# A shared remainder tile's o by heads in array quadrants, one batch's weighted sums placed later, and idle products moved ahead of kv

## The chip, the cores and the metric

The kernel runs on one core of a Trainium2 chip. The metric is device time in microseconds (us) of one launch, the median of several runs. The kernel before takes 321.6 us (three runs, 321.56 to 321.62).

## What is computed

Inputs are q, k and v of 8 batches, 8 heads, 576 positions and a head size of 64, in float32, and the weights of a gated feed-forward layer.

```python
kv = einsum('bhsd,bhse->bhde', k, v)          # 64 x 64 per batch and head
out = einsum('bhsd,bhde->bhse', q, kv)
out = out / sqrt(mean(out**2, -1) + 1e-6) * g_norm
x = out.transpose(0, 2, 1, 3).reshape(4608, 512)
xn = x / sqrt(mean(x**2, -1) + 1e-6) * rms_g
y = (silu(xn @ w_gate) * (xn @ w_val)) @ w_out      # 512 -> 1536 -> 512
```

There is no softmax, so attention is a small product (kv), a product with q (o), and two normings.

## The kernel before

**Tiles.** A batch's 576 positions are four chunks of 128 and a remainder of 64. The remainders of two batches share one tile of 128 rows, so the feed-forward work is nine groups of 512 rows: eight of the batches' chunks (`x`) and one of all remainders (`xr`). The groups run in the order 0 to 6, the remainders' group, 7.

**Feed-forward.** Per group and block j of 128 hidden columns, `gate_of` and `val_of` (L705, L708) each issue four TensorE products over the 512 rows (`mm1`, L694) into one bank of the PSUM pool `mm1`, which has three buffers. ScalarE applies silu (L703), and VectorE multiplies silu by val into `h` (L712). Then come 48 products with `w_out` (`mm2`, L729) for four out tiles in the pool `o2`, each copied by ScalarE (L745) and stored through SyncE's queue (L747).

**Attention of the next batch runs inside a group.** The class `Att` holds its steps: kv (`kv_mm`, L281: each head's product fills half of the array's columns), q transposed by DMA (L342, and L345 for the shared remainder tile), o of the chunks by heads (`o_heads`, L375: contraction over 64 rows, so that each product uses half of the array's rows; two PSUM tiles of `o2` and two of `att` receive the even and the odd heads), and o of the shared remainder tile (`o_rem`, L362: contraction over 128 rows against the block-diagonal `kvs`, one column half per batch, into one tile of `att`). Batches 2, 3, 5 and 7 carry a remainder tile; batches 4 and 6 do not. Then ScalarE squares (`sq_`, L410) and copies (`outa_`, L414) each chunk of o out of PSUM, GpSimd multiplies the square by the norm gain's square (`wsq`, L465), VectorE sums both per head (`red`, L473), computes the row factors in a chain of small steps (`chain`, L512 to L530), and scales o into `xna` (`xna_`, L540). SyncE's queue transposes `xna` into `x` (`x_dma`, L603), in two pieces and one for a remainder.

**What sets the order.** Each group is a list of slots: a slot is one gate group, one val group, or three products of an out tile. A planner (`Placer`, L40) puts each attention step into the first slot where its engine has room by a table of costs, not earlier than the step's inputs allow. `psum` (L66) does so for a TensorE step and also counts the three buffers of `att`: it lets a step into a slot only when the readers of the tiles that it will overwrite have been placed before. `place_attention` (L617) lists a batch's steps; each engine then executes its instructions in the order of the slots. Within `place_attention`, `o_heads` is one step and `o_rem` another, which comes after a tile of `att` is free; the chunks are squared and copied first and the remainder last.

**The start.** Batch 0 is done ahead of the slots, step by step (L854 to L907). `spin` (L243) issues TensorE products of a zero tile that nobody reads: 18 at the start, and four more in the PSUM tile of the first kv products (`kv_pairs`, L286, called at L860). VectorE casts k's first half (L216) and k's remainder `krT` (L858); then `kv_pairs` multiplies k by v (L297), whose loads go through GpSimd's queue.

Of the kernel before, what the change touches and what calls it, by code (L numbers as in the profile page):

```python
# [10 lines left out]
FP32 = mybir.dt.float32  # L11
BF16 = mybir.dt.bfloat16
# [3 lines left out]
ACT = mybir.ActivationFunctionType  # L16
# [71 lines left out]
def kernel(  # L88
# [12 lines left out]
    nc = tc.nc  # L101
    B, H, S, D = q.shape
# [3 lines left out]
    NC = 4  # L106
    MAIN = 128 * NC
# [10 lines left out]
    pool = lambda name, bufs, **kw: ctx.enter_context(tc.tile_pool(name=name, bufs=bufs, **kw))  # L118
# [2 lines left out]
    rstage = pool("rstage", 2)  # L121
    qkv = pool("qkv", 2)
    outa_p = pool("outa", 6)
    sq_p = pool("sq", 3)
    stat = pool("stat", 2)
    sqT_p = pool("sqT", 1)
    xna_p = pool("xna", 2)
# [32 lines left out]
    krT = consts.tile([128, 2, H, D], BF16, name="remk")  # L160
# [82 lines left out]
    def spin(ps, n):  # L243
        for _ in range(n):
            nc.tensor.matmul(ps, lhsT=idle[:, :128], rhs=idle[:, : ps.shape[-1]], start=True, stop=True, skip_group_check=True)  # L245
# [4 lines left out]
    class Att:  # L250
# [103 lines left out]

        def o_rem(self):

            self.o[NC] = o = att_p.tile([128, H, D], FP32, name="att")
            of = (kvs[2], kvs[1]) if self.b == 2 else (kvs[0], kvs[1])
            for j in range(NS):
                for n in range(2):  # L360
                    at = slice(n * REM, (n + 1) * REM)
                    nc.tensor.matmul(  # L362
                        o[at, 2 * j : 2 * j + 2, :], lhsT=self.qTj[:, j, NC, at], rhs=of[n][:, j, :, :],
                        start=True, stop=True, skip_group_check=True,
                    )

        def o_heads(self):

            for n, (pool_, name) in enumerate(((o2_p, "o2"), (o2_p, "o2"), (att_p, "att"), (att_p, "att"))):
                self.o["main", n] = pool_.tile([128, 2, H // 2, D], FP32, name=name)  # L370
            for c in range(NC):
                for j in range(NS):
                    for half in range(2):
                        rows = slice(half * D, (half + 1) * D)
                        nc.tensor.matmul(  # L375
                            self.o["main", c // 2 * 2 + half][:, c % 2, j, :], lhsT=self.qTj[rows, j, c, :],
                            rhs=self.kv[rows, j, half, :], start=True, stop=True, skip_group_check=True,
                        )

        def part(self, t, n):  # L380

            if n >= NC:
                return t[:, n]
            return t[:, n // 2 * 2 : n // 2 * 2 + 2, n % 2 : H : 2]
# [232 lines left out]
    def place_attention(P, b, casts=(), at=0, chain_at=0):  # L617
        a, start = Att(b), at + 2
        V, A = nc.vector, nc.scalar
        N1 = range(a.chunks)  # L620
        P.floor = max(P.floor, at)
        load = P.put("SP", 0.0, a.qT_dma, casts[:1] if b == 2 else casts)
        qt = [("DMA", load[1] + QT_SLOTS)]
        p = P.psum(1.2, lambda: a.kv_mm(ALL), casts)
        kv = [P.reads(P.put("DVE", 0.4, lambda h=h: a.kv_half(h), [p])) for h in range(2)]
        outs, reds = {}, []
        main = P.psum(0.73, a.o_heads, kv + qt, 2)
        for c in N1:
            p = P.psum(0.3, a.o_rem, kv + qt) if c >= NC else main
            s = P.put("ACT", 0.6, lambda c=c: a.sq_(c), [p])  # L630
            outs[c] = P.put("ACT", 0.6, lambda c=c: a.outa_(c), [p])
            if c >= 2:
                P.tiles[-1 if c >= NC else c - 4] += [s, outs[c]]
            assert outs[c][1] < start + 2 * NF, (b, outs)
            w = P.put("POOL", 1.2, lambda c=c: a.wsq(c, nc.gpsimd), [s])
            reds.append(P.put("DVE", 0.68, lambda c=c: a.red(c, 0), [s]))
            reds.append(P.put("DVE", 0.68, lambda c=c: a.red(c, 1), [w]))
        prev = reds
        for n in range(0, 13, 4):
            prev = [P.put("DVE", 0.8, lambda n=n: [f() for f in a.chain(0, a.chunks)[n : n + 4]], prev, chain_at)]  # L640
        xn = [P.put("DVE", 0.68, lambda c=c: a.xna_(c, V), prev + [outs[c]]) for c in N1]
        put = [P.put("SP", 0.0, lambda c=c: a.x_dma(*c), [xn[c[1] - 1]]) for c in ((0, 2), (2, 4), (4, 5))[: a.chunks - 2]]
        return put[2 if b == B - 1 else 1][1] + X_SLOTS
# [178 lines left out]
    P0, P1 = (0, 1), (2, 3)  # L822
# [28 lines left out]
        else:  # L851
            V.tensor_scalar(out=w[:, s], in0=w[:, s], scalar1=gain[:, s : s + 1], scalar2=None, op0=OP.mult)

    spin(mm1_p.tile([128, MAIN], FP32, name="mm1"), 18)  # L854
    a = Att(0)
    cast_main(0, 1, V, H0)
    cast_main(0, 1, A, H1)
    V.tensor_copy(out=krT[: REM // 2], in_=krst.rearrange("p h (c d) -> p c h d", c=2))  # L858
    cast_main(0, 0, V, cs=(0, 2))
    kva = a.kv_pairs(P0, 4)  # L860
    qa, qb = (a.qT_mm(js, (0, 1)) for js in (P0, P1))
    gT = o2_p.tile([128, NS + 1], FP32, name="o2")
    nc.tensor.matmul(gT, lhsT=grow, rhs=identf, is_transpose=True, start=True, stop=True, skip_group_check=True)
# [7 lines left out]
    for half in range(2):  # L871
        rows = slice(half * D, (half + 1) * D)
# [36 lines left out]
    half = MAIN // 2  # L909
# [50 lines left out]
    P = Placer(slots, 3)  # L960
# [64 lines left out]
```

## Time and profile before

| What | us |
|---|---|
| median of three runs | 321.60 |
| the profiled execution | 321.76 |
| its span in the profile | 320.0 |
| VectorE busy | 169.2 |
| ScalarE busy | 138.0 |
| GpSimd busy | 85.2 |

The profile is of one execution. Its span runs from the first to the last recorded instruction; 1.76 us of the execution's time lie around it. Engines are named PE (TensorE), PEld (its weight loads, which overlap its products), DVE (VectorE), ACT (ScalarE), POOL (GpSimd) and SP (SyncE); a name with a q is an engine's own queue of issues. L362 is line 362 of the kernel. The chain that ended last is followed back from the last instruction: at each step to what released it, or to the instruction before it on its engine. In the rows of the chain an engine's pieces join without a gap, so that the starts of two rows show how long everything between them took.

### The profile page before, as it was taken

What the parts mean: (1) busy time and instruction counts of PE and PEld (TensorE: products, weight loads), DVE (VectorE), ACT (ScalarE), POOL (GpSimd) and SP (SyncE); (2) the same over time, 40 slices, a digit from 0 to 9 for tenths busy, and PEclk for the clock granted to TensorE, in tenths of its full rate; (3) what the DMA queues carried; (4) which work ended last, traced back from release to release, by engine and by line L of the source; (5) the groups of instructions that cost most, each with busy time, mean ns of one, the idle gap of its engine ahead of it and who ended that gap; (6) DMA issues with size and microseconds to landing.
All of it is one profiled execution on the core that took longest, in us unless ns stands there. A gap on an engine that the chain in (4) does not pass through costs nothing.

```text
span 320.0 us, 5497 instructions
## 1 busy us (share of the span) xinstructions
PE 312.8 (98%) x2122; PEld 157.7 (49%) x2122; DVE 169.2 (53%) x381; ACT 138.0 (43%) x254; POOL 85.2 (27%) x105
## 2 busy tenths in 40 slices
PE   8799999999999999999999999999999999999995
PEld 3578865444444444444544444444444444444443
DVE  4565536589749651955186717571778043203410
ACT  1465454596667314632383228322842233223321
POOL 8653430077017400830075007500510000000000
PEclk9999999999999999999999999999999999999999
DMA  8999999999761974498349875964000600040002
GB/s 210 221 203 199 195 231 205 228 209 135 153 197 53 166 155 137 131 166 153 121 128 133 148 153 145 153 127 137 11 3 10 183 21 2 15 107 12 0 33 98
DMA packets 79253, 40.69 MB, mean 127 GB/s; under 512 B 42872, under 2 KB 74748, under 8 KB 79228
## 3 DMA queue, kind: packets, MB, share of 16 engines
q0 software_dynamic: 31200, 14.22, 35.1%
q1 hardware_dynamic: 46544, 25.14, 32.2%
q10 hardware_dynamic: 1484, 0.99, 1.0%
q8 instruction: 16, 0.26, 0.3%
q14 instruction: 9, 0.07, 0.1%
HBM read 37.78 MB, written 9.44 MB: 148 GB/s over the span
## 4 chain that ended last, share of the span: by engine, by line
PE 91%; DMA 8%; issue 0%; DVE 0%; ACT 0%; POOLq 0%
PE mm L694 57%; PE o L729 27%; DMA wv<-in_moe_w_val_dram 5%; DMA remv<-in_v_dram 2%; PE att L281 2%; PE mm L729 2%; PE o L375 1%; PE att L375 0%; PE att L362 0%; PE mm L756 0%; PE o L756 0%; PE att L571 0%; PE att L327 0%; PE att L423 0%; PE att L350 0%
## 5 line engine op out<-in xcount | busy, mean ns | idle before, releaser
L712 DVE TENSOR_TENSOR h<-silu,mm 128x512 bf16<-128x512 bf16 (+1 forms) x120 | 75.5, 631 | 86.9 <-PE mm L694 77.0
L703 ACT ACTIVATE silu<-mm 128x512 bf16<-128x512 f32 (+1 forms) x120 | 66.4, 556 | 86.4 <-PE mm L694 75.3
L694 PE MATMUL mm<-x,wv 128*128 128x512 bf16 (+1 forms) x432 | 99.9, 356 | 0.2 <-DMA wv<-in_moe_w_val_dram 0.2
L694 PE MATMUL mm<-x,wg 128*128 128x512 bf16 (+1 forms) x420 | 97.9, 358 | 0.0
L729 PE MATMUL o<-wo,h 128*128 128x512 bf16 x396 | 90.1, 379 | 0.0
L694 PEld LDWEIGHTS <-wv 128*128 128x128 bf16 x480 | 46.2, 98 | 45.7 <-DMA wv<-in_moe_w_val_dram 0.5
L694 PEld LDWEIGHTS <-wg 128*128 128x128 bf16 x468 | 45.1, 98 | 45.7 <-DMA wg<-in_moe_w_gate_dram 0.2
L465 POOL TENSOR_TENSOR sq<-sq,g 128x512 bf16<-128x512 bf16 x28 | 32.0, 1154 | 129.0 <-ACT sq L410 129.0
L729 PEld LDWEIGHTS <-h 128*128 128x128 bf16 x420 | 40.3, 98 | 46.5
L745 ACT COPY osb<-o 128x512 f32<-128x512 f32 x33 | 19.3, 587 | 69.1 <-PE o L729 69.1
L473 DVE TENSOR_REDUCE st<-sq 128x8 f32<-128x512 bf16 x56 | 35.9, 678 | 0.2
L310 DVE CAST kvs<-att 64x256 bf16<-64x256 f32 x14 | 5.9, 422 | 31.9 <-PE att L281 31.7
L540 DVE TENSOR_TENSOR xna<-outa,al 128x512 bf16<-128x512 bf16 x24 | 15.0, 683 | 0.0
L694 PE MATMUL mm<-xr,wg 128*128 128x512 bf16 x48 | 12.3, 379 | 0.0
L694 PE MATMUL mm<-xr,wv 128*128 128x512 bf16 x48 | 12.3, 379 | 0.0
L216 POOL CAST main_q<-stg 128x1024 bf16<-128x1024 f32 (+1 forms) x12 | 11.4, 996 | 1.1 <-DMA stg<-in_q_dram 1.1
L245 PE MATMUL mm<-idle 128*128 128x512 bf16 x27 | 9.0, 505 | 1.2 <-DVE idle L138 1.2
L410 ACT ACTIVATE sq<-att 128x512 bf16<-128x512 f32 x16 | 9.8, 615 | 0.0
L414 ACT CAST outa<-att 128x512 bf16<-128x512 f32 x16 | 9.6, 600 | 0.0
L850 ACT ACTIVATE wv<-wv,gain 128x384 bf16<-128x384 bf16 x16 | 9.0, 608 | 0.4 <-PE mm L694 0.4
L200 POOL DMA_DIRECT2D vc<-in_v_dram x9 | 7.8, 872 | 1.1 <-PE mm L694 1.1
L729 PE MATMUL mm<-wo,h 128*128 128x512 bf16 x24 | 7.8, 379 | 0.0
(132 smaller groups left out, 175.1 us busy)
## 6 DMA issues: line engine op xcount, KB each, us to landing
out_dram<-osb SPq DMA_DIRECT2D x31, 256.0 KB, 2.5
stg<-in_q_dram SPq DMA_DIRECT2D x6, 1024.0 KB, 7.5
vc<-in_v_dram POOLq DMA_DIRECT2D x7, 512.0 KB, 8.2
kc<-in_k_dram POOLq DMA_DIRECT2D x7, 512.0 KB, 6.2
wg<-in_moe_w_gate_dram POOLq DMA_DIRECT2D x4, 384.0 KB, 14.9
wv<-in_moe_w_val_dram POOLq DMA_DIRECT2D x4, 384.0 KB, 16.3
wo<-in_moe_w_out_dram POOLq DMA_DIRECT2D x4, 384.0 KB, 14.7
out_dram<-osb SPq DMA_DIRECT2D x9, 128.0 KB, 2.3
```

Source lines behind the costliest of these rows:

```text
L216: return copy(out=mains[b, t][:, cs[0] : cs[1], h0:h1, :], in_=staged[b, t].rearrange("p h (c d) -> p c h d", c=NC)[:, cs[0] : cs[1], h0:h ...
L245: nc.tensor.matmul(ps, lhsT=idle[:, :128], rhs=idle[:, : ps.shape[-1]], start=True, stop=True, skip_group_check=True)
L410: nc.scalar.activation(out=self.sq[c][:, 0], in_=self.o_of(c), func=ACT.Square)
L414: nc.scalar.copy(out=self.outa[c], in_=self.o_of(c))
L465: eng.tensor_tensor(out=self.sq[c][:, 1], in0=self.sq[c][:, 0], in1=g2, op=OP.mult)
L473: nc.vector.reduce_sum(out=self.part(self.st[:, which], c), in_=of, axis=AX.X)
L540: return eng.tensor_tensor(out=self.part(self.xna, c), in0=self.outa[c].rearrange("p (c h) d -> p c h d", c=2), in1=self.part(self.al, c). ...
L694: nc.tensor.matmul(ps[:, : c1 - c0], lhsT=w[n][:, s, jj * 128 : (jj + 1) * 128], rhs=x_of(g, s, c0, c1), start=s == 0, stop=s == NS - 1)
L703: nc.scalar.activation(out=sis[g, j][:, c0:c1], in_=ps, func=ACT.Silu)
L712: nc.vector.tensor_tensor(out=hs[g, j][:, c0:c1], in0=sis[g, j][:, c0:c1], in1=v_ps, op=OP.mult)
L729: nc.tensor.matmul(ps, lhsT=hs[g, j][:, t * 128 : (t + 1) * 128], rhs=wo[j // OB][:, j % OB, :], start=j == 0, stop=j == NF - 1)
L745: (eng.copy if eng is nc.scalar else eng.tensor_copy)(out=o, in_=ps)
```

## The change

It has three parts.

1. *The remainder's o.* `o_rem` is no step of its own any more: `o_heads` issues it behind the chunks' products. It goes by heads, as these do: sixteen products of 64 rows, 64 columns and 64 moving columns, one for each pair of heads, batch and half, so that the four of a pair lie in the four quadrants of the array. The even heads' results go to a tile of `att`, the odd heads' to a tile of `mm1`. ScalarE squares and copies each half by itself (`sq_rem`, `outa_rem`, 256 wide instead of 512), the half in `mm1` first, and the remainder comes ahead of the chunks on ScalarE, GpSimd and VectorE. A fourth buffer for squares is added.
2. *The third batch (b = 2).* VectorE's sums of the weighted squares are placed three slots later, so other VectorE work goes ahead of them. By the order of the instructions that results, the first eight steps of the chain now stand ahead of the group's last `h`, the second piece of x's transpose behind the store of the second out tile, and one DMA issue of k's remainder ahead of a weighted square on GpSimd. For b = 5 and b = 7 one sum stands behind an `h` that it preceded. TensorE's order is otherwise unchanged.
3. *The start.* All 22 idle products go into one PSUM tile, and five more, 512 wide, take k's cast remainder as moving operand; they stand ahead of kv and so wait for that cast.

```diff
-    sq_p = pool("sq", 3)
+    sq_p = pool("sq", 4)
...
         def o_rem(self):
-            self.o[NC] = o = att_p.tile([128, H, D], FP32, name="att")
             of = (kvs[2], kvs[1]) if self.b == 2 else (kvs[0], kvs[1])
+            self.o[NC] = [
+                pool_.tile([128, H // 2, D], FP32, name=name) for pool_, name in ((att_p, "att"), (mm1_p, "mm1"))
+            ]
             for j in range(NS):
                 for n in range(2):
                     at = slice(n * REM, (n + 1) * REM)
-                    nc.tensor.matmul(
-                        o[at, 2 * j : 2 * j + 2, :], lhsT=self.qTj[:, j, NC, at], rhs=of[n][:, j, :, :],
-                        start=True, stop=True, skip_group_check=True,
-                    )
+                    for half in range(2):
+                        rows = slice(half * D, (half + 1) * D)
+                        nc.tensor.matmul(
+                            self.o[NC][half][at, j, :], lhsT=self.qTj[rows, j, NC, at],
+                            rhs=of[n][rows, j, half, :], start=True, stop=True, skip_group_check=True,
+                        )
+        def sq_rem(self, half):
...
+            nc.scalar.activation(out=self.sq[NC][:, 0, half:H:2, :], in_=self.o[NC][half], func=ACT.Square)
+        def outa_rem(self, half):
...
+            nc.scalar.copy(out=self.outa[NC][:, half:H:2, :], in_=self.o[NC][half])
...
         def o_heads(self):
...
+            if self.chunks > NC:
+                self.o_rem()
...
-        main = P.psum(0.73, a.o_heads, kv + qt, 2)
-        for c in N1:
-            p = P.psum(0.3, a.o_rem, kv + qt) if c >= NC else main
...
+        rem = a.chunks - NC
+        main = P.psum(0.73 + 0.25 * rem, a.o_heads, kv + qt, 2 + rem)
+        for c in (*N1[NC:], *N1[:NC]):
+            if c == NC:
+                for n in (1, 0):
+                    s = P.put("ACT", 0.38, lambda n=n: a.sq_rem(n), [main])
+                    outs[c] = P.put("ACT", 0.38, lambda n=n: a.outa_rem(n), [main])
+                P.tiles[-1] += [s, outs[c]]
...
-            reds.append(P.put("DVE", 0.68, lambda c=c: a.red(c, 1), [w]))
+            reds.append(P.put("DVE", 0.68, lambda c=c: a.red(c, 1), [w], w[1] + 3 * (b == 2)))
...
-    spin(mm1_p.tile([128, MAIN], FP32, name="mm1"), 18)
+    idle_ps = mm1_p.tile([128, MAIN], FP32, name="mm1")
+    spin(idle_ps, 22)
...
-    kva = a.kv_pairs(P0, 4)
+    for _ in range(5):
+        nc.tensor.matmul(
+            idle_ps, lhsT=idle[:, :128], rhs=krT[:, 0].rearrange("p h d -> p (h d)"), start=True, stop=True,
+            skip_group_check=True,
+        )
+    kva = a.kv_pairs(P0)
```

More of the change, by code (lines that the diff above doesn't have):

```diff
@@ L361, in o_rem @@
                     at = slice(n * REM, (n + 1) * REM)
-                    nc.tensor.matmul(
-                        o[at, 2 * j : 2 * j + 2, :], lhsT=self.qTj[:, j, NC, at], rhs=of[n][:, j, :, :],
-                        start=True, stop=True, skip_group_check=True,
-                    )
+                    for half in range(2):
[5 more added lines that the diff above has]
+        def sq_rem(self, half):
+            if NC not in self.sq:
+                self.sq[NC] = sq_p.tile([128, 2, H, D], BF16, name="sq")
+            nc.scalar.activation(out=self.sq[NC][:, 0, half:H:2, :], in_=self.o[NC][half], func=ACT.Square)
+        def outa_rem(self, half):
+            if NC not in self.outa:
+                self.outa[NC] = outa_p.tile([128, H, D], BF16, name="outa")
+            nc.scalar.copy(out=self.outa[NC][:, half:H:2, :], in_=self.o[NC][half])
         def o_heads(self):
@@ L626, in place_attention @@
         outs, reds = {}, []
-        main = P.psum(0.73, a.o_heads, kv + qt, 2)
-        for c in N1:
-            p = P.psum(0.3, a.o_rem, kv + qt) if c >= NC else main
[L630 to L633, printed above, removed]
+        rem = a.chunks - NC
[6 more added lines that the diff above has]
+                P.tiles[-1] += [s, outs[c]]
+            else:
+                s = P.put("ACT", 0.6, lambda c=c: a.sq_(c), [main])
+                outs[c] = P.put("ACT", 0.6, lambda c=c: a.outa_(c), [main])
+                if c >= 2:
+                    P.tiles[c - NC - rem] += [s, outs[c]]
             assert outs[c][1] < start + 2 * NF, (b, outs)
```

## The prediction

> **What bounds the kernel now.** I read the page's busy line first, then the chain of work that ended last, then the PE groups by shape with what ended the idle time before them.
>
> ```profile
> span 320.0 us, 5497 instructions
> PE 312.8 (98%) x2122; PEld 157.7 (49%) x2122; DVE 169.2 (53%) x381; ACT 138.0 (43%) x254; POOL 85.2 (27%) x105
> PE 91%; DMA 8%; issue 0%; DVE 0%; ACT 0%; POOLq 0%
> L694 PE MATMUL mm<-x,wg 128*128 128x512 bf16 x336 | 86.3, 379 | 0.0
> ```
>
> TensorE is busy 98% of the span and holds 91% of the chain; the 8% of DMA is the start. The group of gate products, like the other large groups, waited 0.0 us. So from about 26 us to the tail the time is the sum of what TensorE issues: an edit counts there by the TensorE time it removes, and an edit on another engine counts only if TensorE begins to wait. The chain in order of time shows how closely these rows can be read (start us, us, what):
>
> ```profile
> 8.82 17.15 DMA wv<-in_moe_w_val_dram
> 26.02 1.05 PE mm L694 x8
> ...
> 64.50 0.34 PE o L375 x16
> 64.84 0.23 PE att L375 x16
> 65.08 1.83 PE mm L694 x8
> 66.91 0.34 PE att L362 x8
> 67.26 12.19 PE mm L694 x56
> 79.45 9.71 PE o L729 x45
> 89.16 0.75 PE att L281 x40
> ...
> 90.67 2.59 PE mm L694 x12
> 93.26 0.34 PE o L375 x16
> ...
> 93.83 0.97 PE mm L694 x4
> ...
> 112.52 9.71 PE o L729 x45
> ...
> 126.32 0.34 PE o L375 x16
> ...
> 126.89 18.24 PE mm L694 x84
> 145.13 9.71 PE o L729 x45
> ...
> 254.24 20.72 PE mm L694 x96
> ```
>
> An undisturbed 512-wide product costs 20.72 / 96 = 0.2158 us. The first sixteen products of o by heads take 0.34 us and the next sixteen 0.23: entering a tiled shape of the array costs 0.11. Leaving it costs about as much: 12.19 - 56 x 0.2158 = 0.10 in the row behind L362.
>
> **Part 1, the remainder's o (L362).** Batch b = 3 has a remainder tile, b = 4 has none, and the rest of their work there is the same, 32 products of L375 and 84 of L694 (the 24 groups of four less the three ahead). From the first L375 to the first L729, b = 3 takes 112.52 - 93.26 = 19.26 us and b = 4 takes 145.13 - 126.32 = 18.81. So one remainder block costs 0.45 us: 0.34 in its own row (0.11 to enter, eight 128-wide products, two column halves side by side, in 0.23) and 0.11 to leave. It occurs four times (b = 2, 3, 5, 7): 1.8 us in all.
>
> The new block has 16 products of 64 x 64 in the array's four quadrants, 64 wide, directly behind L375. Leaving the tiled shape is paid by L375 anyway. No row shows four quadrants at once; the nearest show two tiles. L281 does 40 column-half products of 64 columns in 0.75 us: (0.75 - 0.11) / 20 = 0.032 per pair. L375 does 16 row-half products in 0.23: 0.029 per pair. I take the slower rate, since the new weights too are 64 columns wide. If four run side by side, the block is 4 x 0.032 = 0.13 us; if two, 8 x 0.032 = 0.26; if none, 16 x 0.032 = 0.51. To this comes the step from row halves to quadrants, between 0 (it is no new shape to the array) and 0.11 (it costs what each change of shape costs in the rows above). I take four side by side, because column halves and row halves each run abreast here and both banks written are separate, and 0.11, because all changes of shape that the trace has cost that. New block: 0.24. Saved: 0.45 - 0.24 = 0.21 each, 0.84 us for four.
>
> The Trainium skill, "TensorEngine Tiling (Array Packing)", section Tiling Modes (Key Properties), says that changing the tiling mode, and not merely the tile, drains TensorE, which speaks against this change. The trace agrees for 128 x 128 to halves (0.11); from halves to quadrants no run here shows it. By that rule the saving is the 0.84 above; without it, the rival below.
>
> Now the readers. The tile is in two banks, one of the pool att and one of mm1, which has three buffers for the gate and val products. In b = 3 the mm1 half is wanted again two product groups later, 0.10 + 8 x 0.216 = 1.83 us after the block. ScalarE must have squared and copied it by then.
>
> ```profile
> 22.76 0.38 ACT L703 ACTIVATE silu<-mm 128x256 bf16<-128x256 f32 x1 [0.25 <-PE mm L694]
> 93.79 0.61 ACT L850 ACTIVATE wv<-wv,gain 128x384 bf16<-128x384 bf16 x1
> 94.29 0.59 ACT L410 ACTIVATE sq<-o 128x512 bf16<-128x512 f32 x1
> ...
> 78.53 1.94 SPq L345 DMA_TRANSPOSE qTs<-remq  x1
> ```
>
> A half is 256 wide: 0.38 each, 0.76 for both. ScalarE is free at 94.29, where L410 now starts, so the bank is free by 95.05. The block ends at 93.83 + 0.24 = 94.07 and the bank is wanted at 95.9: 0.85 us of cover; if that went, TensorE would wait for the excess. Four pieces of 0.38 in place of two of 0.59 put 0.34 us more on ScalarE per remainder, and it works 43% of the span. Price 0. The remainder's transposed q (issued at 78.53 for b = 3, wanted at 93.8) is long there. The fourth sq buffer costs space only.
>
> **Part 2, b = 2's weighted sums later.** TensorE does not wait in that stretch (64 x 0.216 = 13.82 of the 14.02 us in the two L694 rows, the other 0.20 being two exits), so there is nothing to gain; it can only become late. VectorE, GpSimd and SyncE there:
>
> ```profile
> 66.64 0.60 ACT L850 ACTIVATE wv<-wv,gain 128x384 bf16<-128x384 bf16 x1
> ...
> 65.97 1.15 POOL L465 TENSOR_TENSOR sq<-sq,g 128x512 bf16<-128x512 bf16 x1 [21.15 <-ACT sq L410]
> 69.41 0.73 POOL L196 DMA_DIRECT2D kc<-in_k_dram  x1
> 71.70 3.39 POOL L465 TENSOR_TENSOR sq<-sq,g 128x512 bf16<-128x512 bf16 x3
> ...
> 75.22 1.27 DVE L473 TENSOR_REDUCE st<-sq 128x8 f32<-128x512 bf16 x2
> ...
> 77.00 0.18 DVE L512 TENSOR_SCALAR u<-st 128x40 f32<-128x40 f32 x1
> 78.00 0.68 DVE L712 TENSOR_TENSOR h<-silu,mm 128x512 bf16<-128x512 bf16 x1
> 80.33 0.68 DVE L712 TENSOR_TENSOR h<-silu,mm 128x512 bf16<-128x512 bf16 x1
> ...
> 83.16 2.66 SPq L603 DMA_TRANSPOSE x<-xna  x2
> ...
> DMA to landing us min/median/max: 2.5/3.1/4.9
> ```
>
> On GpSimd the first weighted square (L465) starts at 65.97 now. It would wait for the square of the remainder's second half, which ScalarE does behind the fold of 66.64. The block moves that fold by 0.24 to 66.9, so it ends near 67.4, and the half's square near 67.7. The DMA issue of k's remainder (0.73) goes ahead of the second weighted square instead of behind it. All in all the last weighted square ends near 71.70 + 3.39 + 1.6 = 76.7. Each sum takes 1.27 / 2 = 0.64 us; VectorE's last one ends near 77.8, with a tenth h ahead of it, then comes the eleventh h, and the chain of small steps starts near 78.4, 1.4 us after the 77.00 of now. Its first four steps take 78.00 - 77.00 = 1.0 us; eight of them, some 1.95 us, now run ahead of the twelfth h, which ends at 78.4 + 1.95 + 0.68 = 81.0, as now (80.33 + 0.68). TensorE wants that h for the twelfth product of the first out tile: 79.45 - 0.21 + 11 x 0.216 = 81.6. Cover 0.6 us.
>
> Behind it x's transposes move by the same 1.4 us, and on SyncE's queue the second one comes behind the store of the second out tile as well. The second is issued at 83.16 + 2.66 / 2 = 84.5 now, so near 86.0 (an estimate, with 0.1 for the store). At the median landing of 3.1 it is there at 89.1, at the longest, 4.9, at 90.9. TensorE wants x at 90.67 - 0.21 = 90.46. At the median the cover is 1.4 us and the price 0; at the longest, TensorE waits 0.4 us. GpSimd's issues for v and k of the next batch keep their order among themselves and end long before L281 wants them at 89.16.
>
> **Part 3, the products at the start.**
>
> ```profile
> 8.31 0.68 DVE L858 CAST remk<-stg 32x1024 bf16<-32x1024 f32 x1 [1.87 <-DMA stg<-in_k_dram]
> 10.43 0.38 PE L297 MATMUL mm<-vc,main_k 128*128 128x128 bf16 x4 [1.48 <-DMA vc<-in_v_dram]
> 12.14 0.39 PE L297 MATMUL mm<-vc,main_k 128*128 128x128 bf16 x4
> 14.69 1.24 PE L245 MATMUL mm<-idle 128*128 128x512 bf16 x5
> 26.02 1.05 PE L694 MATMUL mm<-x,wv 128*128 128x256 bf16 x8 [0.23 <-DMA wv<-in_moe_w_val_dram]
> ```
>
> The 18 + 4 idle products are 22 before and after. The five new ones wait for the cast that ends at 8.99; five of that shape took 1.24 us, so they end near 10.3, inside the 1.48 us in which TensorE waits for v until 10.43. They hide in that wait; without it they cost 1.24. The products after the gap run as fast as later ones (0.38 us for four at 10.43, 0.39 at 12.14), so a shorter gap has no rate to win back. And TensorE waits 0.23 us for wv at 26.02, which starts on nothing that changes: a start up to 0.23 us later costs nothing, an earlier one gains nothing. Bounds: nothing to 1.24 - 0.23 = 1.0 us lost, if v were there at the cast already; I take 0, by the row of 10.43.
>
> **The sum.** Against the profiled execution: span 320.0 and 1.76 around it, 321.76. 321.76 - 0.84 = 320.92. The median of the runs shown is 321.60, 0.16 lower, and I predict for that: 321.60 - 0.84 = 320.8 us.
>
> **Rivals.**
> - *Four abreast and no cost for the step to quadrants.* Block 0.13, saved 0.32 each, 1.28: 320.3 us. For it: row halves are kept through the step. Against: every change of shape in the rows cost 0.10 or more.
> - *Two abreast.* Block 0.26 + 0.11 = 0.37, saved 0.08 each, 0.32: 321.3 us, no change that can be told. For it: no row has more than two tiles at work.
> - *One after the other (slower).* Block 0.51 + 0.11 = 0.62, 0.17 lost each: 322.3 us. Its place is the sixteen products; it decides from 0.34 / 16 = 0.021 us per product on. Against it: L375 starts one per 0.014. The Trainium skill, "TensorE: Matmul & The Clock Gate", section "Wait — 56ns, not 53.3ns?", gives about 25 ns as the least distance between two products however narrow; L375's 14 ns disagree for tiles side by side. By that figure an estimate is 16 x 0.025 + 0.11 = 0.51, 0.06 lost each, 321.8 us.
> - *b = 2 late.* x at the longest landing, or the twelfth h over 0.6 us later than I put it: 0.4 us of wait, 320.8 + 0.4 = 321.2 us.
> - *The edit does nothing* because L362 was hidden: against it stands the 0.45 us between b = 3 and b = 4. I give it nothing.
>
> **How the numbers follow.** The measurement tells a change of about 0.2%, 0.64 us, so faster means below 320.96. Forecast 0.45 (of it 0.37 below 320.96, as 0.05 us per block decides), no cost for the step 0.20, two abreast 0.15, one after the other 0.06, b = 2 late 0.08, a later start 0.06 (321.2 to 321.7). Faster: 0.37 + 0.20 + 0.03 = 0.60, the last from small waits in b = 2. Slower: 0.06 + 0.04 of waits over 1.5 us in either late case = 0.10. Within 0.2%: 0.30. The range runs from the no-cost case less 0.1, 320.2, to just over two abreast, 321.4; outside are slower cases and tails, some 0.15.
>
> **What would show it.** In the changed kernel's chain the sixteen quadrant products stand behind the 32 of o by heads, and the way from the first of these to the first out product is 19.05 us in b = 3, with 18.81 kept in b = 4. Entry cost and width are told apart by their row: 0.24 us is the forecast, 0.13 no cost for the step, 0.37 two abreast, 0.62 one by one. The first kv product stays at 10.43 and the first one with x of b = 2 comes at 90.46 with no wait. It is wrong if TensorE has a wait on ScalarE or VectorE in mm1, on x's transpose, or a kv product later than 10.6.

## The result, and the profile after

The changed kernel takes 321.25 us (median of 18 runs, 320.66 to 321.49). The kernel before, run beside it, takes 322.0 us (18 runs, 321.56 to 322.8). The ratio is 0.9973, 95% interval 0.9965 to 0.9981: 0.27% faster. The prediction said 320.8 us in a range of 320.2 to 321.4. The median of the kernel before is higher here than in the three runs shown ahead of the prediction, because its runs form two groups, which those three did not show: 11 of the 18 took 321.56 to 322.11 us (the lower group), the other seven 322.5 to 322.8 (the upper group). The changed kernel has no second group.

The page of the changed kernel: the span is 0.9 us shorter, and so is the profiled execution (320.86 in place of 321.76). It is the third shortest of the 18 runs, so it shows the changed kernel at its better end.

```profile
span 319.1 us, 5569 instructions
PE 311.6 (98%) x2137; PEld 158.4 (50%) x2159; DVE 169.2 (53%) x381; ACT 138.8 (44%) x262; POOL 85.1 (27%) x105
PE 90%; DMA 8%; issue 1%; DVE 0%; ACT 0%; POOLq 0%
```

TensorE still holds the chain. The 1% of "issue" is a set of 0.05 us pieces at places where the trace lacks a record of one matmul; no wait is behind them. The chain in order of time (start us, us, what):

```profile
65.00 0.14 PE att L366
...
65.24 0.32 PE mm L716
...
79.16 7.99 PE o L751 x37
...
90.22 2.75 PE mm L716 x12
92.97 0.34 PE o L389 x16
...
93.54 0.14 PE att L366
...
93.79 18.24 PE mm L716 x84
112.03 0.05 issue
...
125.83 0.34 PE o L389 x16
...
144.64 0.22 PE o L751
```

Line numbers are those of the changed kernel: L389 is o by heads (L375 before), L366 the remainder's products (L362), L716 gate and val (L694), L751 the out products (L729). The block stands between the end of L389 and the next L716: 65.24 - 65.00 = 0.24 us in b = 2 and 93.79 - 93.54 = 0.25 in b = 3, against 0.45 before. In b = 3 the way from the first L389 to the first out product is 112.03 - 92.97 = 19.06 us (the record at 112.03 is missing), where it was 19.26; b = 4, which has no remainder, keeps 144.64 - 125.83 = 18.81.

TensorE's rows of the timeline for b = 3's block (start us, us, what, with the tile written, the part of the array used and the moving operand):

```profile
93.15 0.40 PE L389 MATMUL att<-kvs,qTs 64*128 64x64 bf16 x16
93.47 0.21 PE L366 MATMUL att<-kvs,qTs 64*64 64x64 bf16 x1
...
93.48 0.21 PE L366 MATMUL mm<-kvs,qTs 64*64 64x64 bf16 x1
93.53 0.19 PE L366 MATMUL att<-kvs,qTs 64*64 64x64 bf16 x1
...
93.60 0.19 PE L366 MATMUL mm<-kvs,qTs 64*64 64x64 bf16 x1
93.72 0.61 PE L716 MATMUL mm<-x,wv 128*128 128x512 bf16 x2
```

The first four products, two into each bank, start within 0.01 us, and the next four begin 0.05 us behind them: four quadrants run abreast. All sixteen start within 0.13 us, and the next full-width product 0.12 us behind the last.

The start, from TensorE's timeline:

```profile
9.24 1.24 PE L884 MATMUL mm<-remk,idle 128*128 128x512 bf16 x5 [0.17 <-DVE remk L881]
10.32 0.39 PE L297 MATMUL mm<-vc,main_k 128*128 128x128 bf16 x4
25.94 1.05 PE L716 MATMUL mm<-x,wv 128*128 128x256 bf16 x8 [0.26 <-DMA wv<-in_moe_w_val_dram]
```

b = 2 on VectorE, then on SyncE's queue (start us, time to issue, what):

```profile
78.20 0.46 DVE L528 TENSOR_SCALAR u<-st 128x40 f32<-128x40 f32 x1
...
80.41 0.68 DVE L734 TENSOR_TENSOR h<-silu,mm 128x512 bf16<-128x512 bf16 x1
```

```profile
84.05 1.23 SPq L619 DMA_TRANSPOSE x<-xna  x1
85.38 0.53 SPq L769 DMA_DIRECT2D out_dram<-osb  x1
86.00 1.28 SPq L619 DMA_TRANSPOSE x<-xna  x1
```

The transpose that was issued at 86.00, by itself:

```profile
DMA to landing us min/median/max: 4.2/4.2/4.2
```

The five new products fill the gap ahead of the first kv product, and the first product with wv starts at 25.94 (26.02 before), waiting 0.26 us as before (0.23). So the 0.90 us between the two profiled executions is 0.82 from four blocks and 0.08 from the start. The second piece of x goes out at 86.00 as forecast, but it landed 4.2 us later, at 90.2, and TensorE's first product with it was due there (90.22 in the chain, with one record missing ahead): almost nothing is left of the cover.

### The profile page after: what moved, and what is told of

Its sections match the earlier page's. It is cut to its first block, busy times and chain, and to the rows that moved or that the text cites. A ratio compares the mean times of both kernels' runs of the same rounds, so it can differ in the third digit from the quotient of the medians.

```text
span 319.1 us, 5569 instructions
## 1 busy us (share of the span) xinstructions
PE 311.6 (98%) x2137; PEld 158.4 (50%) x2159; DVE 169.2 (53%) x381; ACT 138.8 (44%) x262; POOL 85.1 (27%) x105
## 4 chain that ended last, share of the span: by engine, by line
PE 90%; DMA 8%; issue 1%; DVE 0%; ACT 0%; POOLq 0%
PE mm L716 57%; PE o L751 27%; DMA wv<-in_moe_w_val_dram 5%; DMA remv<-in_v_dram 2%; PE att L281 2%; PE mm L751 2%; PE o L389 1%; PE att L389 0%; PE mm L778 0%; PE o L778 0%; PE att L587 0%; PE att L327 0%; PE att L366 0%; PE att L439 0%; PE att L350 0%
## 5 line engine op out<-in xcount | busy, mean ns | idle before, releaser
L716 PE MATMUL mm<-x,wv 128*128 128x512 bf16 (+1 forms) x430 | 99.8, 355 | 0.4 <-DMA wv<-in_moe_w_val_dram 0.3
L716 PE MATMUL mm<-x,wg 128*128 128x512 bf16 (+1 forms) x418 | 97.6, 358 | 0.1
L751 PE MATMUL o<-wo,h 128*128 128x512 bf16 x382 | 87.7, 379 | 1.1 <-issue 0.6
L716 PEld LDWEIGHTS <-wv 128*128 128x128 bf16 x480 | 46.2, 98 | 45.7 <-DMA wv<-in_moe_w_val_dram 0.5
L716 PEld LDWEIGHTS <-wg 128*128 128x128 bf16 x468 | 45.4, 98 | 46.3 <-DMA wg<-in_moe_w_gate_dram 0.2
L751 PEld LDWEIGHTS <-h 128*128 128x128 bf16 x420 | 40.3, 98 | 46.5
L716 PE MATMUL mm<-xr,wv 128*128 128x512 bf16 x47 | 12.3, 379 | 0.1
L716 PE MATMUL mm<-xr,wg 128*128 128x512 bf16 x47 | 12.3, 379 | 0.1
L751 PE MATMUL mm<-wo,h 128*128 128x512 bf16 x23 | 7.6, 379 | 0.1
L426 ACT ACTIVATE sq<-att 128x512 bf16<-128x512 f32 x12 | 7.6, 630 | 0.0
L426 ACT ACTIVATE sq<-o 128x512 bf16<-128x512 f32 x12 | 7.3, 610 | 0.0
## 6 DMA issues: line engine op xcount, KB each, us to landing
wo<-in_moe_w_out_dram POOLq DMA_DIRECT2D x4, 384.0 KB, 14.5
```

The lines of the kernel that those rows point to most:

```text
L426: nc.scalar.activation(out=self.sq[c][:, 0], in_=self.o_of(c), func=ACT.Square)
L716: nc.tensor.matmul(ps[:, : c1 - c0], lhsT=w[n][:, s, jj * 128 : (jj + 1) * 128], rhs=x_of(g, s, c0, c1), start=s == 0, stop=s == NS - 1)
L751: nc.tensor.matmul(ps, lhsT=hs[g, j][:, t * 128 : (t + 1) * 128], rhs=wo[j // OB][:, j % OB, :], start=j == 0, stop=j == NF - 1)
```

## The experiments

Three things were open. What part 2 does: a guard that part 1 needs (theory A), or a step that only costs (theory B). Why the block takes 0.24 us. And whether part 3, which I had put at nothing, removes the second group of runs (theory C). All runs stand beside runs of the kernel before on the same chip.

**Part 1 alone, parts 1 and 2, part 3 alone.** In each diff of this section "-" is the full change, unless another kernel is named. The first hunk undoes part 2, the second part 3; part 1 alone has both, parts 1 and 2 the second. Part 3 alone is the kernel before with part 3 of the change put in.

```diff
-            reds.append(P.put("DVE", 0.68, lambda c=c: a.red(c, 1), [w], w[1] + 3 * (b == 2)))
+            reds.append(P.put("DVE", 0.68, lambda c=c: a.red(c, 1), [w]))
...
-    idle_ps = mm1_p.tile([128, MAIN], FP32, name="mm1")
-    spin(idle_ps, 22)
+    spin(mm1_p.tile([128, MAIN], FP32, name="mm1"), 18)
...
-    for _ in range(5):
-        nc.tensor.matmul(
-            idle_ps, lhsT=idle[:, :128], rhs=krT[:, 0].rearrange("p h d -> p (h d)"), start=True, stop=True,
-            skip_group_check=True,
-        )
-    kva = a.kv_pairs(P0)
+    kva = a.kv_pairs(P0, 4)
```

> Part 1 alone: the remainder's o by heads in quadrants behind the chunks' o, with the sums of b = 2 and the start as before. Theory A (the gain is TensorE time of the four blocks; part 2 only guards it): each block costs 0.25 us in place of 0.45, so -0.8 us, but without the later sums VectorE stands in b = 2 before GpSimd's weighted square of the first chunk, which ends near 71.7 in the changed kernel, so that an h and with it a PSUM bank of mm1 come late: 0.4 to 1.2 us of TensorE wait between 70 and 76 us, and in all 0 to -0.4 us against before (ratio 0.999 to 1.000). Theory B (part 2 does nothing at all): -0.8 us, ratio 0.9975, no wait of TensorE in b = 2.

> Parts 1 and 2 with the start as before (no products on k's remainder). Theory A (the start is hidden behind v and then behind wv): the same time as the changed kernel, ratio 0.9973 within 0.001, and the first kv product and the first product on the third piece of wv at the same times within 0.15 us. Theory C (the products at the start are worth something that the one profile does not show, such as a faster clock behind them in some runs): 0.3 us or more above the changed kernel, with runs that spread more widely.

> Part 3 alone on the kernel before: 22 idle products in one tile and five on k's cast remainder ahead of kv. Theory A: no change, ratio 1.000 within 0.001; the five products lie between the cast's end and v's landing. Theory C: 0.3 us or more faster than before.

Part 1 alone: 322.26 us (11 runs, 321.7 to 323.06), ratio 1.0013 [1.0001, 1.0025]. Its block is 0.25 us, as in the full change, and yet nothing is won. The chain of its profile in b = 2:

```profile
65.44 0.32 PE mm L716
...
72.56 0.69 DVE h L734
...
73.29 4.26 PE mm L716 x19
...
80.36 1.73 PE o L751 x8
```

An h stands on the chain in the middle of TensorE's products. VectorE's row ahead of it says why (in brackets its idle time and what ended it):

```profile
71.96 0.69 DVE L489 TENSOR_REDUCE st<-sq 128x8 f32<-128x512 bf16 x1 [0.88 <-POOL sq L481]
```

VectorE waits 0.88 us in a sum for GpSimd's weighted square, and the h behind it, whose end frees a buffer of `mm1`, comes late. From the block to the first out product it takes 80.36 - 65.44 = 14.92 us; in the full change 79.16 - 65.24 = 13.92. So part 1 without part 2 gives 1.0 us back in one place. Theory A holds: part 2's work is to put other VectorE work ahead of those sums. The total is above the 0.999 to 1.000 that I expected of it.

Parts 1 and 2: 321.53 us (12 runs: seven from 321.24 to 321.56, five from 322.17 to 322.6), ratio 0.9994 [0.9981, 1.0007]. Its profile has the block at 0.25 us and a wait:

```profile
86.19 4.54 DMA x<-xna
...
90.78 2.75 PE mm L716 x12
93.53 0.34 PE o L389 x16
```

x is late. From the first wv product, 26.13 there, to b = 3's o by heads it takes 67.40 us; in the full change 92.97 - 25.94 = 67.03. So 0.37 us are lost to the transpose.

Part 3 alone: 321.69 us (11 runs, 321.52 to 321.85), ratio 0.9991 [0.9982, 0.9999]. None of its runs falls in the upper group, though 11 of the 35 runs of the kernel before beside it do (322.32 to 322.73). That speaks for theory C and against my price of 0.

**The block's order, one quadrant at a time.** The same sixteen products, with the loop over j innermost, so that four of one quadrant follow each other in the program.

```diff
-            for j in range(NS):
-                for n in range(2):
...
-                    for half in range(2):
+            for n in range(2):
...
+                for half in range(2):
+                    for j in range(NS):
```

> The changed kernel with the loops of the remainder's products turned round: four products in a row on the same quadrant of the array, then the next quadrant; the same 16 products, weights and readers. Theory A (the block is cheap because four quadrants work side by side): the block grows from 0.25 us to between 0.45 (neighbouring quadrants overlap at the seams) and 0.63 (16 x 0.032 + 0.11), so 0.8 to 1.5 us slower than the changed kernel, ratio to before 1.000 to 1.002. Rival (the block's time is its entry and the issue of 32 instructions, in whatever order): unchanged, ratio 0.9973.

321.19 us (12 runs, 320.76 to 321.78), ratio 0.9979 [0.9969, 0.9989]. The block takes 0.27 to 0.28 us, not 0.45 or more. TensorE's rows of b = 5:

```profile
158.78 0.21 PE L366 MATMUL att<-kvs,qTs 64*64 64x64 bf16 x1
158.79 0.21 PE L366 MATMUL mm<-kvs,qTs 64*64 64x64 bf16 x1
158.81 0.21 PE L366 MATMUL att<-kvs,qTs 64*64 64x64 bf16 x1
...
158.94 0.19 PE L366 MATMUL mm<-kvs,qTs 64*64 64x64 bf16 x1
159.06 0.39 PE L716 MATMUL mm<-x,wv 128*128 128x512 bf16 x1
```

The program has four products into `att`, then four into `mm`, and so on; the records alternate between the two, 0.013 us apart. So, by these records, products of different quadrants start out of program order, and the order inside the block costs 0.02 to 0.03 us at most. My expectation of a serial block falls.

**All in one quadrant.** Here the remainder's o is computed from the even heads and the first batch only, all sixteen products in one quadrant; ScalarE then reads 64 partitions twice, in eight instructions in place of four.

```diff
-                    at = slice(n * REM, (n + 1) * REM)
+                    at = slice(0, REM)
...
-                        rows = slice(half * D, (half + 1) * D)
+                        rows = slice(0, D)
...
```

> The changed kernel with all 16 products of the remainder's o sent through one quadrant of the array (rows 0 to 63, columns 0 to 63); ScalarE reads those 64 partitions twice. So the remainder's o is that of the even heads and the first batch only, everywhere. Theory A (four quadrants side by side make the block cheap): one product per 0.027 to 0.032 us, the block costs 0.54 to 0.62 us in place of 0.25, 1.2 to 1.5 us slower than the changed kernel, ratio to before 1.001 to 1.002. Rival (the block is bound by entry and issue, whichever quadrant the products go to): the block stays at 0.25 to 0.30, ratio 0.9973.

```profile
65.12 0.21 PE L366 MATMUL att<-kvs,qTs 64*64 64x64 bf16 x1
65.17 0.19 PE L366 MATMUL mm<-kvs,qTs 64*64 64x64 bf16 x1
...
65.61 0.19 PE L366 MATMUL mm<-kvs,qTs 64*64 64x64 bf16 x1
65.74 0.60 PE L722 MATMUL mm<-x,wg 128*128 128x512 bf16 x2
```

One product each 0.03 us: (65.61 - 65.17) / 14 = 0.031. From the first product to the next full-width one it takes 65.74 - 65.12 = 0.62 us, where the full change takes 93.72 - 93.47 = 0.25: the difference is the abreastness. The price of a serial block that the third rival had is thus real; the change does not pay it. The total, 326.46 us (4 runs), ratio 1.0131 [1.0115, 1.0148], says nothing of the block: four times 0.37 us is 1.5 us of it, and the rest comes from ScalarE, whose extra pieces put it on the chain. Its rows:

```profile
65.84 0.76 ACT L376 ACTIVATE sq<-mm 64x256 bf16<-64x256 f32 x2 [0.39 <-PE mm L366]
```

Each piece of half the partitions costs 0.38 us, as one of all 128 does (0.37 in the changed kernel), so the half in `mm1` takes about 1.5 us to read in place of 0.75, and the cover that part 1 has there is gone.

**The remainder in row halves.** The same products with 64 rows and all 128 columns, in the shape of o by heads, so that the array's shape does not change behind the chunks.

```diff
...
-                            self.o[NC][half][at, j, :], lhsT=self.qTj[rows, j, NC, at],
+                            self.o[NC][half][:, n, j, :], lhsT=self.qTj[rows, j, NC, :],
...
```

> The remainder's o in the shape of o by heads: sixteen products of 64 rows with all 128 columns as weights, so that the array's shape doesn't change behind o of the chunks; the results of both batches stand in four planes, and ScalarE reads each half in two pieces of 64 partitions (eight instructions in place of four), so the total is not comparable and only the block's row is read. If the 0.12 us at the entry is the step from row halves to quadrants: no such step, the block is 16 x 0.0145 = 0.23 us, its products one every 0.0145 us from the first on. If the 0.12 comes with any new weights or tiles: 0.35 us.

```profile
64.56 0.40 PE L394 MATMUL att<-kvs,qTs 64*128 64x64 bf16 x16
64.79 0.19 PE L365 MATMUL att<-kvs,qTs 64*128 64x64 bf16 x1
...
65.12 1.04 PE L721 MATMUL mm<-x,wg 128*128 128x512 bf16 x4
```

From the start of the sixteen chunk products to the first of the remainder it takes 64.79 - 64.56 = 0.23 us, which is just what those sixteen take; in the changed kernel it is 93.47 - 93.15 = 0.32. So the step into quadrants costs 0.09 us, and it is missing where the shape stays. Up to the next full-width product both blocks come out alike, though: 65.12 - 64.56 = 0.56 here and 93.72 - 93.15 = 0.57 there. What four abreast win over two in the row halves, the step takes back. So the 0.2 us that a block saves on TensorE do not hang on the quadrants: row halves behind the chunks give the same. Whether the old eight products, moved to that place, would do so too was not run. Its total, 324.94 us (one run), has ScalarE's eight pieces in it like the run before.

**Where x goes out, and when the sums come.** In one kernel VectorE's folds of two weights come 10 and 5 slots later, so that both pieces of x are transposed ahead of the second store; in the other the sums of b = 2 come six slots later in place of three.

```diff
-                        f = P.put(eng, cost * FB[n], lambda w=w, n=n, j=j, e=eng: fold(w[n], j, e), at=starts[1] + at + j)
+                        f = P.put(eng, cost * FB[n], lambda w=w, n=n, j=j, e=eng: fold(w[n], j, e), at=starts[1] + at + j + (10 if eng == "DVE" and n == 1 else 5 if eng == "DVE" and n == 2 else 0))
```

and

```diff
-            reds.append(P.put("DVE", 0.68, lambda c=c: a.red(c, 1), [w], w[1] + 3 * (b == 2)))
+            reds.append(P.put("DVE", 0.68, lambda c=c: a.red(c, 1), [w], w[1] + 6 * (b == 2)))
```

> The changed kernel, with VectorE's folds of the norm gain into the second and third pieces of w_gate placed ten and five slots later in group 1, so that the five xna of b = 2 follow the chain without a gap and both transposes of x go ahead of the store of the second out tile. Theory D (in most executions of the changed kernel x of b = 2 lands after TensorE wants it, which costs 0.3 to 0.5 us): x lands 1.5 us earlier, the wait is gone, 0.3 to 0.5 us below the changed kernel, ratio to before 0.9955 to 0.9965, and its runs lie within 0.4 us. Rival (x is in time, and the changed kernel's runs spread for another reason): ratio 0.9973 and the same spread.

> The changed kernel with the sums of the weighted squares of b = 2 six slots later in place of three. Theory D: the chain of small steps starts about three slots, 2.6 us, later, and so does x's second piece, which lands near 92.5; TensorE waits for it 2 to 3 us at the start of the third group (near 90.4), ratio to before 1.003 to 1.006. Theory A in its first form (x has 1.4 us of cover): 0.5 to 1.5 us of wait, ratio 0.999 to 1.002.

x earlier: 321.03 us (5 runs, 320.81 to 321.18), ratio 0.9961 [0.9946, 0.9976]. Its transposes are issued from 83.42 on and TensorE has no wait in that stretch (26.10 to 93.13, 67.03 us). It beats the kernel before, and it is the lowest median of all, though its interval overlaps that of the full change.

Sums later still: 322.21 us (10 runs, 321.67 to 322.9), ratio 0.9998 [0.9986, 1.001]. The whole gain is gone:

```profile
89.06 3.14 DMA x<-xna
...
92.24 2.76 PE mm L716 x12
95.00 0.34 PE o L389 x16
```

From 26.36 to 95.00 are 68.64 us in place of 67.03: 1.6 us more, of which 1.3 are one wait of TensorE for x. That is less than theory D had (2 to 3 us) and a little more than its rival (0.5 to 1.5). So part 2 lies in a narrow window: without it TensorE loses 1.0 us to an h, with twice of it 1.6 us, mostly to x.

**Part 2 alone.** Only the sums of b = 2 three slots later, on the kernel before.

> Only b = 2's weighted sums three slots later; block and start are those of the kernel before. Theory C (part 2 gives nothing by itself: it is the guard that part 1 needs; the upper group of runs belongs to the start): no TensorE time goes, so 321.5 to 322.1 us in about two thirds of the runs and some 0.9 us more in the others, median within 0.2% of the kernel before; x's second piece lands 4.2 us or more after its issue, so that TensorE waits 0 to 0.4 us for it ahead of b = 3's o by heads. Rival A (the prediction's price of 0, at the median landing): no wait for x at all, the same distribution as before. Rival B (the later sums gain by themselves): the median falls by 0.3 us or more.

321.82 us (11 runs: eight from 321.56 to 321.89, three from 322.49 to 322.87), ratio 1.0006 [0.9995, 1.0017]. In its profile x is on the chain:

```profile
85.85 4.73 DMA x<-xna
...
93.37 0.34 PE o L375 x16
```

From 25.92 to 93.37 are 67.45 us, where the kernel before takes 93.26 - 26.02 = 67.24: 0.21 us of wait. Part 2 wins nothing by itself and costs up to that much.

**The pause ahead of kv.** To test theory C, one kernel is the changed one without the five products on k's remainder and with 16 idle products in place of 22; another is the kernel before with two idle products fewer; a third is the kernel before once more, for a second profile.

```diff
-    spin(idle_ps, 22)
+    spin(idle_ps, 16)
...
-    for _ in range(5):
-        nc.tensor.matmul(
-            idle_ps, lhsT=idle[:, :128], rhs=krT[:, 0].rearrange("p h d -> p (h d)"), start=True, stop=True,
-            skip_group_check=True,
-        )
```

and, against the kernel before,

```diff
-    spin(mm1_p.tile([128, MAIN], FP32, name="mm1"), 18)
+    spin(mm1_p.tile([128, MAIN], FP32, name="mm1"), 16)
```

> The changed kernel without the five products on k's remainder and with 16 idle products in place of 22, so that TensorE stands still for about 2.7 us ahead of the first kv product. Theory C (a pause there lets the array's clock drop, in some executions after a pause of 1.5 us and in most after 2.7 us, and the start behind it then runs at half rate): the first kv products come one per 0.107 us in place of 0.054, the first product on the third piece of wv comes up to 1 us later, 0.6 to 1.2 us slower than the changed kernel in most runs. Theory A (TensorE waits there anyway, and the rate behind the pause is the full one): the same time as the changed kernel, ratio 0.9973.

> The kernel before with 16 idle products ahead of kv in place of 18 in the first loop, nothing else, so that TensorE pauses about 0.6 to 0.9 us longer ahead of the first kv product (2.1 to 2.4 us in place of 1.48). Theory C (a pause ahead of kv lets TensorE's rate drop about 1 us after it, the more often the longer it is): over half of the runs in the upper group, median 322.3 to 322.8 us; a profiled run of that group shows eight products of L316 in about 1.0 us in place of 0.61 and the four kv products near 12 us in 0.6 in place of 0.39. Rival D (the upper group comes from somewhere else, the loads for instance): the share of the upper group stays near a third and the median near 321.9 us.

> The kernel before once more, for a profile: if this run falls in the upper group (322.3 us or more, a chance of a third), theory C expects eight products of L316 near 11 us in about 1.0 us in place of 0.61, and the first product with x of the first group at 26.6 or later in place of 26.02 with no wait for wv; rival D expects the same start as in the profile at hand and the time lost later. If it falls in the lower group: the start as in the profile at hand.

The long pause: 322.38 us (12 runs, 321.34 to 324.19), ratio 1.0011 [0.9995, 1.0027]. Its profile:

```profile
10.12 0.38 PE L297 MATMUL mm<-vc,main_k 128*128 128x128 bf16 x4 [3.78 <-DMA vc<-in_v_dram]
...
11.03 1.00 PE L316 MATMUL att<-ident,main_q 128*128 128x128 bf16 x8
...
12.16 0.61 PE L297 MATMUL mm<-vc,main_k 128*128 128x128 bf16 x4
```

After a pause of 3.78 us the first four products run at 0.38 us, not at the half rate from the first product on that I expected; about 1 us later eight of L316 take 1.00 us (0.61 or 0.62 in every other profile) and four of L297 0.61 (0.39). The clock that TensorE was granted shows it too. In these rows (a stretch in us, its length, then the busy time of each engine) it is the third number from the end, and 1.00 is full:

```profile
10.00:11.00 1.00, 0.83 (x12) 0.65 (x11) 0.71 (x2) 0.14 (x1) 0.64 (x1) 1.00 1.43 196
...
12.00:13.00 1.00, 1.00 (x11) 0.98 (x11) 0.81 (x4) 0.22 (x1) 1.00 (x3) 0.50 1.23 220
```

The clock is 0.50 from about 11.1 to 14.5 us, and full before and behind that. The first row of sixteen gate products starts at 28.90, where it starts at 27.94 in the kernel before: 0.96 us were lost. So a pause can cost TensorE rate, and it shows only after the first products. (x takes 4.96 us to land in this profile, and TensorE waits 0.6 us for it as well.)

Two products fewer: 321.61 us (10 runs, two of them in the upper group at 322.39 and 322.48), ratio 0.9992 [0.998, 1.0004]; the profile has a pause of 2.55 us and L316 at 0.61 us. The kernel before once more: 321.59 us (one run), a pause of 2.03 us, L316 at 0.61.

The granted clock also tells the two groups of runs apart. Over the whole span, 3.4 us at half clock make a mean of 0.995. That is the mean of the profiled execution with the long pause (322.8 us), and of all 43 upper-group runs of the other kernels whose clock is on record; the runs outside the group have 0.998 or more. The distance between the groups fits as well: in the comparison with the changed kernel the medians of the kernel before's two groups are 321.72 and 322.67, 0.95 us apart. So an upper-group run loses as much clock as the profile with the long pause does. Where in the run it loses it was seen only there: the six other profiles of starts without the five products (the kernel before twice, part 1, parts 1 and 2, part 2, two products fewer) are of lower-group runs.

Whether a longer pause makes the group more frequent is not settled. With two products fewer I expected over half of the runs in it; 2 of 10 are, against 9 of 21 beside them, which so few runs cannot tell apart. With the long pause 9 of 12 have a clock of 0.995 or less, against 9 of 23. The pause also differs from execution to execution (1.06 to 2.10 us in the five profiles with 18 idle products in the first loop and none on k's remainder), and it is known for profiled ones alone.

What stands is a count. Without the five products, 23 of 56 runs of five kernels and 36 of 97 of the kernel before are in the upper group; with them none of 61 runs of seven kernels has such a clock. That part 3 removes the group is shown, and that the group's runs are those with a lower granted clock. Which piece of part 3 does it, the products that fill the pause or the other place of the idle ones, stays open.

## Why the prediction was right, and where it was not

**The bound.** Right. TensorE holds 90% of the chain after, 91% before, and what the profiled executions lost in the experiments, they lost in waits of TensorE that the chain names, but for the 0.96 us of halved clock behind the long pause.

**The block.** Right, in its size and in its working: forecast 4 x 0.032 + 0.11 = 0.24 us, measured 0.24 and 0.25; forecast 19.05 us from the first o by heads to the first out product in b = 3, measured 19.06. Four abreast is shown by the rows (four starts within 0.01 us) and by the kernel with one quadrant (0.62 us in place of 0.25). That the step from row halves to quadrants costs is shown by the kernel in row halves, in which it is missing. The rivals "no cost for the step" and "two abreast" fall; the slower rival's 0.62 us is what one quadrant costs, and the change uses four. The Trainium skill's 25 ns as the least distance between two products ("TensorE: Matmul & The Clock Gate", "Wait — 56ns, not 53.3ns?") does not hold across quadrants, where sixteen start within 0.13 us; within one quadrant, at 31 ns each, nothing here contradicts it.

**Readers of the remainder.** Right. ScalarE reads the half in `mm1` first and nothing on TensorE waits for it:

```profile
94.27 0.37 ACT L379 CAST outa<-mm 128x256 bf16<-128x256 f32 x1
```

The bank is free at 94.64 (forecast 95.05) and wanted at 95.46, when the third product group behind the block starts. Where the pieces double, in the two kernels with eight of them, the cover is gone and TensorE waits.

**Part 2.** The times were right: the chain of small steps starts at 78.20 (forecast 78.4), the twelfth h ends at 81.09 (81.0), x's second piece is issued at 86.00 (86.0). The step that failed is the landing: I took the median of all of x's transposes, 3.1 us, and a cover of 1.4 us. This piece takes 4.2 us in the full change, 4.54 with parts 1 and 2, 4.73 with part 2 alone: the cover is 0.2 us or less. x is on the chain in three profiles with part 2 as in the change, with 0.4 us of wait in parts 1 and 2, 0.2 in part 2 alone and 0.6 in the long pause, and not in two (the full change, one quadrant at a time); in the two kernels with eight pieces on ScalarE it is there too. That is the mechanism and the size of the rival "b = 2 late", to which I gave 0.08. The other error is in what the part is for: I wrote that there was nothing to gain, which holds for the kernel before (part 2 alone: 1.0006), but part 1 alone would lose 1.0 us to an h behind a sum that waits for GpSimd. I had followed when GpSimd ends its weighted squares, and not what VectorE's queue would do with the sums left where they stood.

**Part 3.** The price of 0 was wrong: part 3 gains. I argued from one profile, in which the products after the gap run at full speed, that there was "no rate to win back". That profile is of a lower-group run, with a mean clock of 1.000. Part 3 alone takes 0.1% off the median (0.9991), by removing the upper group.

**The sum.** The forecast saving was 0.84 us of 321.60, 0.26%; measured were 0.27%. That agreement is luck, two errors that cancel. The medians differ by 322.0 - 321.25 = 0.75 us. Against the kernel before's lower group alone the difference is 321.72 - 321.25 = 0.47 us, little over half of the forecast; the other 0.28 us are the upper group, which I had not seen and which part 3 removes (0.0009 x 322 = 0.3 us in its own comparison). The blocks do give 0.82 us in the profiles, so in the median run something takes 0.3 to 0.4 us back. The absolute number, 320.8, missed 321.25 by 0.45 us: I subtracted from a median of three runs, all of the lower group and 0.12 us below its median here, and left x's waits out. The median lies where the rival "b = 2 late" put it, 321.2. That waits for x make up the whole shortfall is likely but not shown: with x earlier the median is 321.03, but its interval overlaps, and the one profile of the changed kernel has no such wait, with 0.2 us of cover or less.

## What to carry over

- When a change moves a transfer, price its landing at the long end of its rows, not at the median of all of them; cover worked out from the median was 1.2 us too large here.
- Read every part of a change for what the others do to it: part 2 is worthless alone (1.0006), and part 1 without it is slower than before (1.0013).
- Three runs can all be of one group. Where many runs can be had, look at how they spread before the median of a few is used as a base, and before one profile is used to say that there is nothing to win. The granted clock of each run told the groups apart here, 0.995 against 0.998 and more, and its value in a stretch of the trace told what the mean over the span hid.

## What the runs showed of the hardware that was not expected

- Products in different quadrants start out of program order: with four of one quadrant behind each other in the program, the records alternate between two banks 0.013 us apart, and the block takes 0.27 to 0.28 us.
- A change of the array's shape costs about 0.1 us also between two tiled shapes (row halves to quadrants), and no such step is there when the shape stays.
- After a pause of 3.78 us TensorE's first products run at full rate and those about 1 us later at about half of it (1.00 us in place of 0.61): the granted clock is 0.50 for 3.4 us, from 11.1 to 14.5 us. After 2.55 us and less no profile here shows that. The mean clock of all 43 upper-group runs on record, 0.995, is what 3.4 us at half clock give.
- The second piece of x's transpose of b = 2 landed after 3.3 us in the profiles of the kernels with neither part 1 nor part 2, and after 4.1 to 5.0 us in nine of the ten kernels with part 1 or part 2. Its time in the queue does not explain it: with x earlier it is issued at 84.7, 0.2 us later than in the kernel before, and lands after 4.6 us; with the sums later still it is issued at 89.06 and lands after 3.1 us. What sets it was not tried.
